# One visit of TensorE for the key-value products of two pairs of heads

## The chip, the cores and the metric

The kernel runs on one core of one Trainium2 chip. The metric is device time in microseconds (us), taken as the median of the timed runs. The profile shows one execution of the program; its engines are named PE (TensorE, the matrix engine; PEld is its loading of the stationary operand), DVE (VectorE), ACT (ScalarE), POOL (GpSimd) and SP (SyncE, which here only issues transfers).

## The reference, cut to what matters

Linear attention is followed by a two-layer network over all tokens:

```
q_s = softmax of q over the 64 numbers of a head
k_s = softmax of k over the 576 keys of a head
kv  = einsum('bhsd,bhse->bhde', k_s, v)          # 64 x 64 per head
x   = einsum('bhsd,bhde->bhse', q_s, kv)         # 8 batches x 576 tokens, 8 heads
h   = x @ w_in
out = (h * clip(h + 3, 0, 6) / 6) @ w_out        # 4608 x 512 -> 2048 -> 512
```

All is float32. There are 8 batches, 8 heads of 64 numbers and 576 keys per batch.

## The kernel before, in words

**Blocks.** The 4608 tokens are worked through in nine blocks of 512 (`j` from 0 to 8). A block's attention gives `x`, kept as a rounded half and a remainder (`split`: ACT casts, DVE subtracts), since a float32 product is made of three products of such halves. Blocks 0 and 1 use the plain first product (`gemm1`); from block 2 on (`FAST`) the first product follows a scheme with seven quarter products (`fast_pair`, one call for two of the sixteen column blocks of `w_in`, so eight "pairs of columns" per block), for which `x_factors` prepares sums of `x` and `fast_weights` once prepares sums of the weights.

**Attention.** A unit of attention is one pair of heads of one block (`attention(j, hp)`, four units per block: 128 rows hold two heads of 64). It is a Python generator of four steps, separated by `yield`: (1) load, take the maximum of each key row (`km`) and make q's softmax on its transposed layout (`q_softmax_t`), ending with a transpose on DVE; (2) spread the maxima: POOL copies the column `km` to a 128x128 tile `kb`, PE transposes it into `pm`, DVE subtracts it from `ke`, ACT takes the exponential, and q is split; (3) `kv_of`: ten products of 64 columns on PE into `pkv` (five chunks of keys, two heads), then DVE divides by the sum of the exponentials, which is a 65th column of the product, and the result is split; (4) six products into `px` give `x`, which `x_factors` copies and splits. The last chunk of keys has 64 rows (`TAIL`), the four others 128. With 576 keys and blocks of 512 tokens, a block needs the `kv` of batch `j - 1` and of batch `j`. There are eight batches, so block 8 has no step (3).

**What sets the order.** The generator `steps` is advanced once per column block in blocks 0 and 1 and twice per pair of columns from block 2 on (in `fast_pair`, at the second and fourth call of `slot`). It runs ahead: during block `j` it does mostly the attention of block `j + 1`. Units come in the order 0, 2, 1, 3, since `x_factors` needs pair 2 for pair 0 and pair 3 for pair 1. From block 1 on PE executes its instructions in the order in which they are written; on the other engines a scheduler sets the order, with priority for the evacuations marked `high_priority`. The second product of an earlier pair of columns (`gemm2`, into `po`) waits in `pend` and is issued in fills of 4, 7, 7 and 6 between the quarter products. Transfers are issued by SP in one queue; among them are the weights of the fast scheme (`w<-wf`), through a ring of twelve half tiles.

**Names in the profile.** The matmul helper has one line, L91, so its groups are told apart by tile: `pkv` (step 3), `px` (step 4), `pm` (transposes, L97), `ph` and `pz` (first product), `po` (second product). L123 and L124 are the two halves of `split`. L353 is the subtraction of the maxima, L340 the POOL copy to `kb`, L215 to L218 the division, L535, L541 and L554 evacuations of the first product.

## Time and profile before

| what | value |
|---|---|
| time, median of 3 runs | 892.73 us (892.33 to 893.6) |
| the profiled execution: first to last instruction | 888.9 us |
| PE busy, share of the span | 858.4 us, 97% |
| PEld, DVE, ACT, POOL busy | 739.2, 614.6, 464.8, 132.9 us |
| products into `pkv` in blocks 1 to 7 | 560 instructions, 28 visits of 20 |
| transposes into `pm` | 24 |

The execution behind the profile has no time of its own beside its span; the span lies 3.8 us below the median of the timed runs, which also hold what comes before the first and after the last instruction. A line of `kv_of` that issues one product stands as two instructions in the profile, so ten products are a visit of 20. Ends of matmuls are modelled by the profile, since they are pipelined; starts are what can be compared. Rows of the timeline merge neighbours of one kind: start, time to the last end, engine, line, tiles, shape, count.

### The profile page before, as it was taken

The numbers are of one execution on the slowest core, as the hardware profiler recorded it, in microseconds if no ns is written. First come the engines' busy times: TensorE is split into PE (matmuls) and PEld (weight loads), VectorE is DVE, ScalarE is ACT, GpSimd is POOL, SyncE is SP. The second block draws the span as 40 slices with busy tenths as digits, with TensorE's granted clock in tenths as the row PEclk, the third lists the DMA queues.
The fourth block names the chain that finished last, engine by engine and source line by source line (L and its number), as shares of the span: only waits on it lengthen the run. The fifth ranks groups of instructions, "written<-read, shape, count | busy, mean of one in ns | idle before, by whom it ended". The sixth has DMA issues, their size and how long they took to land.

```text
span 888.9 us, 15262 instructions
## 1 busy us (share of the span) xinstructions
PE 858.4 (97%) x5380; PEld 739.2 (83%) x5380; DVE 614.6 (69%) x1266; ACT 464.8 (52%) x944; POOL 132.9 (15%) x329
## 2 busy tenths in 40 slices
PE   5799998999999999999999999999999999999998
PEld 3578776787789888888888888888888888889896
DVE  7999867899777766767585757676867565444333
ACT  7998753544445454545454545444554554434333
POOL 5000132021212110202020202021212120100000
PEclk9899999999999999999999999999999999999999
DMA  9992583538487668676777668676755575567541
GB/s 372 413 369 84 125 203 136 180 108 289 161 259 224 219 202 258 216 224 203 228 233 229 209 220 259 200 230 195 256 158 183 161 230 170 167 178 224 170 140 47
DMA packets 98474, 185.19 MB, mean 208 GB/s; under 512 B 9824, under 2 KB 24160, under 8 KB 96352
## 3 DMA queue, kind: packets, MB, share of 16 engines
q1 hardware_dynamic: 96192, 180.03, 62.3%
q0 software_dynamic: 1632, 3.15, 2.0%
q10 hardware_dynamic: 576, 1.05, 0.3%
q8 instruction: 43, 0.70, 0.3%
q14 instruction: 31, 0.25, 0.1%
HBM read 156.93 MB, written 24.12 MB: 204 GB/s over the span
## 4 chain that ended last, share of the span: by engine, by line
PE 83%; DVE 7%; DMA 6%; ACT 2%; issue 1%; POOL 0%; SPq 0%; ACTq 0%; DVEq 0%; POOLq 0%
PE po L91 41%; PE ph L91 33%; PE pz L91 4%; PE px L91 2%; PE pkv L91 2%; DMA w<-v 2%; DMA qt<-in_qf_dram 2%; DVE w L124 1%; DMA out_dram<-ob 1%; DVE v L155 1%; DVE v L149 0%; DMA wf<-w 0%; POOL swap L289 0%; DVE km L267 0%; DVE v L159 0%
## 5 line engine op out<-in xcount | busy, mean ns | idle before, releaser
L91 PE MATMUL po<-w,w 128*128 128x512 f32 x1008 | 260.8, 394 | 0.8 <-ACT w L123 0.8
L91 PEld LDWEIGHTS po<-w,w 128*128 128x128 f32 x1008 | 178.4, 189 | 30.7 <-ACT w L123 1.1
L91 PE MATMUL ph<-x_lo,w 128*128 128x256 f32 (+1 forms) x800 | 152.2, 305 | 2.7 <-DVE x_lo L124 2.3
L91 PEld LDWEIGHTS ph<-w,w 128*128 128x128 f32 x1008 | 133.8, 190 | 11.0 <-DVE second L535 1.4
L91 PE MATMUL ph<-x_hi,w 128*128 128x256 f32 (+1 forms) x592 | 138.4, 338 | 4.4 <-DMA w<-v 3.3
L91 PE MATMUL ph<-w,w 128*128 128x256 f32 x1008 | 140.4, 284 | 1.2 <-DVE second L535 1.2
L91 PEld LDWEIGHTS ph<-x_lo,w 128*128 128x128 f32 x800 | 117.0, 189 | 17.0 <-DVE x_lo L124 2.6
L91 PEld LDWEIGHTS ph<-x_hi,w 128*128 128x128 f32 x592 | 93.3, 191 | 18.8 <-DMA w<-v 3.5
L124 DVE TENSOR_TENSOR w<-g,w 128x512 fp32r<-128x512 f32 x112 | 77.2, 689 | 35.3 <-ACT w L123 35.3
L123 ACT CAST w<-g 128x512 fp32r<-128x512 f32 x112 | 69.4, 619 | 56.7 <-DVE g L541 34.4
L91 PE MATMUL po<-w 128*128 128x512 f32 x336 | 86.7, 394 | 0.1
L91 PEld LDWEIGHTS po<-w 128*128 128x128 f32 x336 | 59.4, 188 | 10.8 <-ACT w L123 0.5
L91 PE MATMUL po<-w,g_hi 128*128 128x512 f32 x256 | 67.4, 401 | 0.9 <-ACT g_hi L123 0.9
L556 ACT ACTIVATE g<-second,three 128x512 f32<-128x512 f32 x56 | 40.5, 724 | 33.9 <-DVE second L554 26.5
L91 PEld LDWEIGHTS po<-w,g_hi 128*128 128x128 f32 x256 | 47.7, 190 | 12.2 <-ACT g_hi L123 1.4
L540 ACT ACTIVATE g<-ph,three 128x256 f32<-128x256 f32 x56 | 26.6, 474 | 57.9 <-PE ph L91 57.9
L541 DVE SCALAR_TENSOR_TENSOR g<-g,ph 128x256 f32<-128x256 f32 x56 | 23.2, 415 | 47.1 <-ACT g L540 47.0
L534 ACT COPY second<-ph 128x256 f32<-128x256 f32 x56 | 20.8, 372 | 63.1 <-PE ph L91 63.1
L557 DVE SCALAR_TENSOR_TENSOR g<-g,second 128x512 f32<-128x512 f32 x56 | 39.0, 697 | 15.3 <-ACT g L556 15.2
L91 PE MATMUL pz<-x_hi,w 128*128 128x256 f32 x336 | 49.5, 283 | 0.0
L535 DVE TENSOR_TENSOR second<-second,ph 128x256 f32<-128x256 f32 x56 | 23.1, 413 | 37.5 <-ACT second L534 37.5
L289 POOL COPY swap<-qr 32x16 f32<-32x16 f32 x112 | 30.6, 273 | 96.4 <-DVE qr L301 92.8
(125 smaller groups left out, 1264.2 us busy)
## 6 DMA issues: line engine op xcount, KB each, us to landing
w<-wf SPq DMA_DIRECT2D x392, 256.0 KB, 3.0
raw<-in_w_dram SPq DMA_DIRECT2D x16, 1024.0 KB, 13.4
out_dram<-ob SPq DMA_DIRECT2D x36, 256.0 KB, 3.3
vt<-in_v_dram SPq DMA_DIRECT2D x28, 325.0 KB, 3.5
wf<-w SPq DMA_DIRECT2D x16, 512.0 KB, 4.7
kt<-in_kT_dram SPq DMA_DIRECT2D x28, 288.0 KB, 3.0
ke<-in_k_dram SPq DMA_DIRECT2D x24, 320.0 KB, 2.9
qt<-in_qf_dram SPq DMA_DIRECT2D x28, 256.0 KB, 3.0
```

The source lines that it names most:

```text
L91: nc.tensor.matmul(out, lhsT, rhs, start=start, stop=stop, skip_group_check=goes_on)
L123: nc.scalar.copy(hi, src)
L124: engine.tensor_sub(lo, src, hi.bitcast(F32))
L155: nc.vector.scalar_tensor_tensor(vu, high, 0xC0000000, m, op0=ALU.bitwise_and, op1=ALU.bitwise_or)
L289: nc.gpsimd.tensor_copy(swap[r : r + QD], stat[o : o + QD])
L534: nc.scalar.copy(second[:, HT:], x)
L535: nc.vector.tensor_add(second[:, HT:], second[:, HT:], y)
L540: nc.scalar.activation(r[:, HT:], x, AF.Relu, bias=three, scale=1.0)
L541: nc.vector.scalar_tensor_tensor(r[:, HT:], r[:, HT:], 6.0, x, op0=ALU.min, op1=ALU.mult)
L556: nc.scalar.activation(r, second, AF.Relu, bias=three, scale=1.0)
L557: nc.vector.scalar_tensor_tensor(r, r, 6.0, second, op0=ALU.min, op1=ALU.mult)
```

## The change

From block 2 on, attention is written for two pairs of heads at a time, (0, 2) and then (1, 3), in the generator `paired`, with eight steps where two units had four each. In the order of the steps: load and softmax of the first pair; its maxima and exponentials, and load and softmax of the second; maxima and exponentials of the second; q of the first transposed and split; `kv` of both pairs in one visit of PE, the second pair 128 columns further in the same tile; `x` of the first; q of the second transposed and split; `x` of the second. In block 2 itself the eight steps are six. The last chunk of keys is used with all 128 rows: the loaded `ke` and `vt` of blocks 2 to 7 already have rows below the 64 keys (the smallest float in k, zeros in v), and in blocks 0 and 1 POOL now writes zeros there. The column of maxima is no longer copied to a tile: PE's transpose reads the column with a step of zero. The sum plus epsilon and its reciprocal are taken once for both pairs. The split halves of `kv` have six buffers where they had five.

```diff
-    def kv_of(j, hp, ke, vt):
+    def kv_of(j, units):
+        n = len(units)
         pkv = ps_a.tile([P, TB], F32, name="pkv", tag="pa")
-        for c in range(NCH):
-            r = slice(0, P if c < NC4 else TAIL)
-            for h in range(2):
-                hs = slice(h * D, (h + 1) * D)
-                mm(pkv[hs, 0 : D + 1], ke[r, c, hs], vt[r, c, h, :], c == 0, c == NCH - 1)
-        rk = att.tile([P, 1], F32, name="rk", bufs=2)
-        nc.vector.tensor_scalar_add(rk, pkv[:, D : D + 1], EPS)
+        for i, (hp, ke, vt) in enumerate(units):
+            for c in range(NCH):
+                for h in range(2):
+                    hs = slice(h * D, (h + 1) * D)
+                    mm(
+                        pkv[hs, i * KVW : i * KVW + D + 1],
+                        ke[:, c, hs],
+                        vt[:, c, h, :],
+                        c == 0,
+                        c == NCH - 1,
+                        i > 0,
+                    )
+        sums = pkv.rearrange("p (i n) -> p i n", n=KVW)[:, 0:n, D]
+        rk = att.tile([P, 2], F32, name="rk", bufs=2)[:, 0:n]
+        nc.vector.tensor_scalar_add(rk, sums, EPS)
         nc.vector.reciprocal(rk, rk)
...
     def k_softmax(j, km, ke, kt):
         nc.scalar.copy(ke[0:TAIL, NC4], pe2[0:TAIL, 0:P])
+        nc.gpsimd.memset(ke[TAIL:P, NC4], 0.0)
...
+    def paired(j, hps):
+        qts, kes, kbs, vts = {}, {}, {}, {}
+        def begin(hp):
...
+            if j < B:
+                km = att.tile([P, 1], F32, name="km", bufs=2)
+                nc.vector.tensor_reduce(km, kt, axis=AX.X, op=ALU.max)
+                kbs[hp] = km.broadcast_to([P, P])
+            q_softmax_t(qts[hp])
+        def exp_k(hp):
+            if j < B:
+                ke = kes[hp]
+                pm = ps_a.tile([P, TB], F32, name="pm", tag="pa")
+                flip(pm[:, 0:P], kbs[hp])
...
+        def turn_q(hp):
+            qT = moe.tile([P, 2 * DM], F32, name="m", tag="v", bufs=3)[:, 0:TB]
+            nc.vector.transpose(qT, qts[hp])
...
+        one, two = hps
+        begin(one)
+        yield
+        exp_k(one)
+        begin(two)
+        yield
+        exp_k(two)
+        yield
+        turned = turn_q(one)
+        if j > FAST:
+            yield
+        if j < B:
+            kv_of(j, [(hp, kes[hp], vts[hp]) for hp in hps])
+            for hp in hps:
+                kv_split(j, hp)
+        yield
+        x_of(one, *turned)
+        if j > FAST:
+            yield
+        turned = turn_q(two)
+        yield
+        x_of(two, *turned)
...
     def steps():
-        for j in range(1, NB):
-            heads = range(NP) if j < FAST else (0, 2, 1, 3)
-            for hp in heads:
-                unit = attention(j, hp)
...
+        for hp in range(NP):
+            for _ in attention(1, hp):
+                yield
+            yield
+        for j in range(FAST, NB):
+            for hps in ((0, 2), (1, 3)):
+                for _ in paired(j, hps):
                     yield
-                next(unit, None)
+                yield
```

The first two places are on PE and DVE. On PE, during block 2, where step (3) of a unit of block 3 stood (`w` and `x_hi`, `x_lo` are operands of the first product, `po` is a fill of the second product), this stood before:

```order
L91 MATMUL po<-w_533,w_1016 128x512 x6
L91 MATMUL ph<-x_lo_311,w_656 128x256 x6
L91 MATMUL po<-w_533,w_1016 128x512 x6
L91 MATMUL pkv<-vt,ke 64x65 x10
L91 MATMUL ph<-w_365,w_656 128x256 x6
L91 MATMUL pz<-x_hi_310,w_716 128x256 x6
L91 MATMUL ph<-x_hi_310,w_716 128x256 x6
```

And now, for both pairs of heads (1, 3):

```order
L91 MATMUL ph<-w_337,w_782 128x256 x6
L91 MATMUL ph<-w_309,w_782 128x256 x6
L91 MATMUL po<-w_593,w_1075 128x512 x7
L91 MATMUL pkv<-vt,ke 64x65 x20
L91 MATMUL ph<-x_lo_315,w_835 128x256 x6
L91 MATMUL po<-w_593,w_1075 128x512
```

Twenty products stand in a row where ten stood, once per two pairs of heads, and they come after the first fill of seven of a pair of columns and not after its fill of six.

On DVE, in the first pair of columns of block 3, between two evacuations of the first product (`second`) and the split of its result (`w`), this stood before (`qt`, `qm` and `m` belong to the softmax of the next unit, `ob` is a store of block 2):

```order
L535 TENSOR_TENSOR second<-second,ph 128x256
L124 TENSOR_TENSOR qT_lo<-m,qT_hi 128x512
L604 TENSOR_SCALAR ob<-po 128x512
L124 TENSOR_TENSOR x_lo_311<-v,x_lo_311 128x256
L307 STREAM_TRANSPOSE m<-qt 128x512
L297 TENSOR_REDUCE qm<-qt 128x16
L541 SCALAR_TENSOR_TENSOR g<-g,ph 128x256
L554 TENSOR_TENSOR second<-second,ph 128x256
L290 TENSOR_TENSOR qm<-qm,swap 128x16
L124 TENSOR_TENSOR w_957<-g,w_957 128x512
```

And now:

```order
L571 TENSOR_TENSOR second<-second,ph 128x256
L124 TENSOR_TENSOR kv_lo_0_3508<-kv,kv_hi_0_3507 128x128
L124 TENSOR_TENSOR kv_lo_2_3512<-kv,kv_hi_2_3511 128x128
L640 TENSOR_SCALAR ob<-po 128x512
L577 SCALAR_TENSOR_TENSOR g<-g,ph 128x256
L124 TENSOR_TENSOR w_964<-g,w_964 128x512
L399 STREAM_TRANSPOSE m<-qt 128x512
L590 TENSOR_TENSOR second<-second,ph 128x256
```

Ahead of the evacuation into `g` (L541, now L577) stood five other operations after `second`; now three stand there, two of them on 128x128, and the transpose has moved behind the split.

The third place is on DVE in the next pair of columns of block 3, from the split of its first result (`w_1075` in the changed program) to that of its second. Before, at the next like place, the work beside the first product was that of two softmaxes alone:

```order
L124 TENSOR_TENSOR w_957<-g,w_957 128x512
L299 TENSOR_TENSOR qt<-qt,qm 128x512
L297 TENSOR_REDUCE qm<-qt 128x16
L557 SCALAR_TENSOR_TENSOR g<-g,second 128x512
L527 TENSOR_TENSOR first<-first,pz 128x256
L301 TENSOR_REDUCE qr<-qt 128x16
L124 TENSOR_TENSOR w_1016<-g,w_1016 128x512
```

And now:

```order
L124 TENSOR_TENSOR w_1075<-g,w_1075 128x512
L320 TENSOR_TENSOR qt<-qt,qr 128x512
L314 TENSOR_TENSOR qt<-qt,qm 128x512
L590 TENSOR_TENSOR second<-second,ph 128x256
L124 TENSOR_TENSOR qT_lo<-m,qT_hi 128x512
L124 TENSOR_TENSOR x_hi_314<-v,x_hi_314 128x256
L124 TENSOR_TENSOR x_lo_315<-v,x_lo_315 128x256
L124 TENSOR_TENSOR w_309<-v,w_309 128x256
L563 TENSOR_TENSOR first<-first,pz 128x256
L124 TENSOR_TENSOR w_337<-v,w_337 128x256
L316 TENSOR_REDUCE qr<-qt 128x16
L593 SCALAR_TENSOR_TENSOR g<-g,second 128x512
```

The splits of `x_factors` (`x_hi`, `x_lo`, `w_309`, `w_337`) now stand among the softmaxes of the two next pairs of heads, ahead of L593, whose result the split into `w` waits for.

More of the change, by code (lines that the diff above doesn't have):

```diff
@@ L305, in q_softmax_t @@
         nc.vector.tensor_mul(qs, qs, across(qr))
-        qT = moe.tile([P, 2 * DM], F32, name="m", tag="v", bufs=3)[:, 0:TB]
-        nc.vector.transpose(qT, qt)
-        return qT
     def attention(j, hp):
-        early = j < 2
         if not j:
@@ L357, in attention @@
-        if early:
-            pool, tag = (ps_a, "pa") if j else (ps_o, "po")
-            tp = pool.tile([P, TB], F32, name="tp", tag=tag)
-            for c in range(NC4):
-                flip(tp[:, c * P : (c + 1) * P], qt[:, c].rearrange("p h d -> p (h d)"))
-            if j:
-                qT = att.tile([P, TB], F32, name="qT", tag="qT_hi")
-            nc.scalar.copy(qT, tp)
-        else:
-            qT_hi = att.tile([P, TB], F32R, name="qT_hi")
-            qT_lo = att.tile([P, TB], F32R, name="qT_lo")
-            split(qT_hi, qT_lo, qT)
@@ L369, in attention @@
[L369 to L375 removed]
+            kt = att.tile([P, S], F32, name="kt", bufs=1)
+            nc.sync.dma_start(kt, kT[j, hp])
+            ke = att.tile([P, NCH, P], F32, name="ke", bufs=2)
+            vt = att.tile([P, NCH, 2, D + 1], F32, name="vt", bufs=2)
+            nc.sync.dma_start(vt, v[j, hp])
+            qt = att.tile([P, TB], F32, name="qt", bufs=2)
+            nc.sync.dma_start(qt, q[j, hp])
@@ new lines, in attention @@
+            qt = qt.rearrange("p (c h d) -> p c h d", c=NC4, h=2)
+        km = att.tile([P, 1], F32, name="km", bufs=2)
+        ks = k_softmax(j, km, ke, kt)
+        next(ks)
+        q_softmax(qt, j == 1, nc.vector if j else nc.gpsimd)
+        yield
+        next(ks, None)
+        pool, tag = (ps_a, "pa") if j else (ps_o, "po")
+        tp = pool.tile([P, TB], F32, name="tp", tag=tag)
+        for c in range(NC4):
+            flip(tp[:, c * P : (c + 1) * P], qt[:, c].rearrange("p h d -> p (h d)"))
@@ L378, in attention @@
+        if j:
+            qT = att.tile([P, TB], F32, name="qT", tag="qT_hi")
+        nc.scalar.copy(qT, tp)
+        yield
+        kv_of(j, [(hp, ke, vt)])
+        yield
         pool, tag = (ps_a, "pa") if j else (ps_h, "ph")
@@ L390, in attention @@
                     mm(px[:, c], kv_lo, qT_hi[:, c], False, True)
-        if j < FAST:
-            x_hi, x_lo = x_block(j)
-            split(x_hi[:, hp, :], x_lo[:, hp, :], px)
-            if j == 1:
-                kv_split(j, hp)
-        else:
-            x_factors(j, hp, px)
+            x_factors(j, hp, px)
+        one, two = hps
[9 more added lines that the diff above has]
+            yield
+        if j < B:
+            kv_of(j, [(hp, kes[hp], vts[hp]) for hp in hps])
+            for hp in hps:
+                kv_split(j, hp)
+        yield
[5 more added lines that the diff above has]
+        x_of(two, *turned)
     HT = TB // 2
@@ L636, in steps @@
     def steps():
-        for j in range(1, NB):
-            heads = range(NP) if j < FAST else (0, 2, 1, 3)
-            for hp in heads:
-                unit = attention(j, hp)
-                for step in range(4):
-                    next(unit, None)
-                    if j == FAST and step == 3 and hp != 3:
-                        continue
+        for hp in range(NP):
[5 more added lines that the diff above has]
+                for _ in paired(j, hps):
                     yield
-                next(unit, None)
+                yield
     step = steps()
```

99 lines of the change are left out of this document (45 added, 54 removed).

## The prediction

> **What bounds the kernel now.** I read the page first: busy shares, the slices, and the chain that ended last.
>
> ```profile
> span 888.9 us, 15262 instructions
> PE 858.4 (97%) x5380; PEld 739.2 (83%) x5380; DVE 614.6 (69%) x1266; ACT 464.8 (52%) x944; POOL 132.9 (15%) x329
> ...
> PE   5799998999999999999999999999999999999998
> ...
> DVE  7999867899777766767585757676867565444333
> PE 83%; DVE 7%; DMA 6%; ACT 2%; issue 1%; POOL 0%; SPq 0%; ACTq 0%; DVEq 0%; POOLq 0%
> ```
>
> PE is full but for the first slices, and 83% of the chain is PE. A share of busy time hides how stages differ, so I read the stages next (columns: stretch, then busy us and count of PE, PEld, DVE, ACT, POOL, the granted clock, DMA share, GB/s).
>
> ```profile
> 0.00:33.00 33.00, 17.83 (x124) 11.52 (x124) 27.92 (x51) 27.01 (x39) 11.32 (x19) 0.89 0.97 385
> 33.00:144.00 111.00, 102.79 (x504) 80.61 (x504) 99.52 (x159) 83.40 (x166) 14.13 (x27) 0.97 0.69 217
> ...
> 430.00:522.70 92.70, 92.41 (x638) 82.04 (x637) 64.42 (x144) 46.61 (x100) 15.77 (x44) 1.00 0.70 223
> ```
>
> Up to 144 us DVE and ACT feed PE and it waits for them; from there on PE sets the pace (92.41 of 92.70 us) and DVE has some 28 us to spare in a block. So in blocks 2 to 8 what PE is spared is spared at the end, as long as nothing else gets late. The waits of PE confirm it (columns: total, times, longest):
>
> ```profile
> PE ph L91 <- DMA w<-v: 3.3, 2, 3.0
> ...
> PE ph L91 <- DVE second L535: 1.2, 1, 1.2
> ...
> PE po L91 <- ACT w L123: 0.8, 1, 0.8
> ...
> PE ph L91 <- ACT second L534: 0.4, 1, 0.4
> PE ph L91 <- DVE g L541: 0.3, 1, 0.3
> ```
>
> The last four belong to blocks 2 and later, 2.7 us in all.
>
> **The visit to `pkv`.** Its price is read from starts. The timeline of PE with no visit, then with one at the same place between a fill and the products after it:
>
> ```profile
> 300.27 1.55 PE L91 MATMUL po<-w,w 128*128 128x512 f32 x6
> 301.66 0.86 PE L91 MATMUL ph<-w,w 128*128 128x256 f32 x6
> 302.36 0.87 PE L91 MATMUL pz<-x_hi,w 128*128 128x256 f32 x6
> ...
> 310.91 1.55 PE L91 MATMUL po<-w,w 128*128 128x512 f32 x6
> 312.39 0.95 PE L91 MATMUL pkv<-vt,ke 128*64 128x65 f32 x20
> 313.27 0.98 PE L91 MATMUL ph<-w,w 128*128 128x256 f32 x6
> 314.08 0.88 PE L91 MATMUL pz<-x_hi,w 128*128 128x256 f32 x6
> ```
>
> Six `po` take 1.39 us to the next start without a visit and 1.48 before one: entry 0.09. The visit takes 312.39 to 313.27, 0.88. The six products behind it take 0.81 and not 0.70: exit 0.11. Sum 1.08. Where the 0.88 goes, narrower stretches of the same view and the view by tile show:
>
> ```profile
> 312.39 0.28 PE L91 MATMUL pkv<-vt,ke 128*64 128x65 f32 x2
> ...
> 312.50 0.40 PE L91 MATMUL pkv<-vt,ke 128*64 128x65 f32 x8
> ...
> 312.79 0.29 PE L91 MATMUL pkv<-vt,ke 128*64 128x65 f32 x4
> ...
> 313.01 0.33 PE L91 MATMUL pkv<-vt,ke 64*64 64x65 f32 x4
> ...
> L91 PE MATMUL pkv<-vt,ke x20: 218/222/271, 312.4 to 313.1; 128*64 128x65 f32 x16, 64*64 64x65 f32 x4
> ...
>   issue: 7.1, 21
> ```
>
> The two heads run side by side, so twenty instructions are ten couples. The first takes 0.11 (312.39 to 312.50). The last four of the sixteen with 128 rows begin at 312.79, so five couples lie between 312.50 and 312.79: 0.058 each. Couple eight would begin at 312.85 and the 64-row ones begin at 313.01: 0.16 and not 0.058, so the change of shape costs 0.10. The two 64-row couples take 0.26 to the exit and not 0.12: 0.05 for a first couple again, 0.10 on the way back to 128x128. "issue", 21 times in all visits, says that PE waits there for nothing else that the trace shows.
>
> **What the change does to it.** A visit for two pairs is one first couple, 18 at 0.058 and a last one with its way out at 0.16: 0.11 + 1.04 + 0.16 = 1.31, plus entry and exit 0.20: 1.51. Two visits are 2.16 now. Saved 0.65 per two pairs; blocks 2 to 7 have two such visits each, twelve: **7.8 us**. The fifth chunk's added rows cost nothing by this count: 64-row products last 0.22 as the others do, and the rows are loaded already. In blocks 0 and 1 a visit loses only its change of shape, 0.15; the four in block 1's attention give **0.6**, the four before 33 us nothing, since PE is busy there 17.83 of 33 us. The one visit waits for the exponentials of both pairs, and so does what is behind it on PE, in order. They are asked for two and more steps earlier, a step being half a pair of columns, 5.3 us (10.55 us for a pair of columns without attention, below), so I take no wait.
>
> The order of DVE moves the other stalls. At the start of block 3 PE waits for a split:
>
> ```profile
> 345.97 0.68 DVE L604 TENSOR_SCALAR ob<-po 128x512 f32<-128x512 f32 x1
> ...
> 346.90 0.70 DVE L307 STREAM_TRANSPOSE m<-qt 128x512 f32<-128x512 f32 x1
> 347.54 0.69 DVE L297 TENSOR_REDUCE qm<-qt 128x16 f32<-128x512 f32 x1
> 348.14 0.41 DVE L541 SCALAR_TENSOR_TENSOR g<-g,ph 128x256 f32<-128x256 f32 x1
> ...
> 349.04 0.87 PE L91 MATMUL ph<-x_hi,w 128*128 128x256 f32 x6
> 350.68 0.74 PE L91 MATMUL po<-w,w 128*128 128x512 f32 x2 [0.77 <-ACT w L123]
> ```
>
> L541 stands behind a store, a transpose and a maximum of the next unit. In the changed order the transpose and that softmax are behind it, so this wait should go. At the start of block 2 the same waits, 1.2 and 0.4, pull the clock down as well:
>
> ```profile
> 252.00:258.00 6.00, 4.76 (x26) 4.46 (x26) 4.89 (x12) 2.59 (x6) 1.77 (x5) 0.72 0.81 233
> ...
> 254.94 1.48 PE L91 MATMUL pz<-x_hi,w 128*128 128x256 f32 x6
> 256.22 1.48 PE L91 MATMUL ph<-x_hi,w 128*128 128x256 f32 x6
> ```
>
> Six `pz` take 1.28 to the next start, where six products took 0.70 above. PE's 4.76 us at a clock of 0.72 would be 3.4 at full clock: 1.3 lost. The waits and the clock are 4.0 us that can go. At block 2 a store of the previous block still stands ahead of L571, so I take **3.0**, between 0 (each wait replaced by another) and 4.0.
>
> The Trainium skill, page "TensorE: Matmul & The Clock Gate", Part 1, has the clock fall back to half only after an idle window of about 3.4 us. By that the short waits at block 2 would cost no clock, 1.3 us less could be won, and the sum below would be 882.6. This case's trace does not agree: 0.72 after waits of 1.2 and 0.4.
>
> **Edits taken at nothing.** The POOL copies (24) and twelve additions and reciprocals less on DVE free engines that PE covers; if DVE were the bound, 12 x 0.31 = 3.7 us more would come (the rows of `rk` are 152 and 156 ns). Transposing a column with step zero is not in this trace:
>
> ```profile
> L97 PE MATMUL pm<-ident,kb 128*128 128x128 f32 x24 | 6.5, 271 | 0.0
> L97 PEld LDWEIGHTS pm<-ident,kb 128*128 128x128 f32 x24 | 3.3, 139 | 1.0
> ```
>
> Nearest is the same load from a full tile, 139 ns under running products: 0. If the load took three times as long and nothing covered it, 24 x 0.28 = 6.7. I take 0, since the same number of elements is read. A gain is excluded: the load is hidden now. The eight zero fills on POOL (15% busy) go between its transfers `w<-v`, one of which a PE wait of 3.0 names; with the new order of the first two blocks, where DVE and ACT lead, I take 0 and keep 3 us either way.
>
> SP's queue is re-dealt: the key transfers of two pairs come one step apart and the second waits for the first's maximum, with weight fetches behind it. The ring holds twelve of them, 12/7 of a pair of columns or 18 us of work, against one softmax, some 5 us.
>
> Sum, against the profiled execution: 888.9 - 7.8 - 0.6 - 3.0 = 877.5. The median of the runs lies 3.8 above that span and I carry it over: **881.3 us**.
>
> **Rivals.**
>
> (a) *Only the visits pay.* Other waits replace those at the block starts, and the new order of the DVE-led start costs up to 3: 892.7 - 8.4 = 884.3, to 887.3. For it: the scheduler re-deals those blocks, and before 144 us PE idles 23 us (33.00 - 17.83 and 111.00 - 102.79), so an order there can be worth some of it. Against it: the order at the start of block 3 above.
>
> (b) *DVE becomes the bound where `x_factors` meets two softmaxes* (the third place of the order). Stretches of a pair of columns each, the last without attention:
>
> ```profile
> 580.52:592.24 11.72, 11.72 (x89) 10.24 (x88) 10.04 (x23) 6.28 (x12) 3.29 (x14) 1.00 0.66 211
> 592.24:603.66 11.42, 11.42 (x74) 10.29 (x73) 8.32 (x21) 5.96 (x15) 3.65 (x7) 1.00 0.68 214
> 826.15:836.70 10.55, 10.55 (x69) 9.50 (x68) 3.92 (x9) 3.97 (x8) 0.00 (x0) 1.00 0.58 175
> ```
>
> The fullest two hold 18.4 us of DVE in 23.1 and PE has no wait there. The change packs in about as much, the two softmaxes and the six splits of `x_factors` closer together, and without a visit two pairs of columns last as little as 21.1 (2 x 10.55). If the split for the second product gets late by d, PE waits d twelve times; the gain of 11.4 is gone at d = 0.95, and at 1.5 the time is 892.7 + 6.6 = 899. Against it: 21.1 - 18.4, some 2.7 us of room.
>
> By the Trainium skill, page "TensorEngine Tiling (Array Packing)", PSUM Bottleneck, packing speeds TensorE but not the evacuation, which may then become the bottleneck. That speaks for (b); the rows show no such wait yet.
>
> (c) *The change of shape is not what is paid.* Should the 0.1 steps at entry, at 64 rows and at exit come from something per unit, two pairs would still cost 2.16 and only the block starts change: 889.7 to 892.7. The step-zero load at its upper end lands in the same place as (a), 888.
>
> **How the numbers follow.** Forecast 0.54 (879 to 884), rival (a) 0.27 (884 to 889), (c) 0.08, (b) 0.11, most of it slower than before. The likeliest time is 881.3. Two cases in ten left out, one at each end: 877.0 (all 4.0, and the start 3 better: 877.3) to 889.5. What a measurement of this kernel can tell from no change is about 0.2%, 1.8 us: faster 0.85 (forecast, (a) and half of (c)), same 0.07 (the rest of (c), a small (b)), slower 0.08.
>
> **What would show it.** Right: in blocks 2 to 7 twelve visits of 40 instructions, 1.31 us from first start to the next product, all of 128 rows, 0.058 a couple; at the start of blocks 2 and 3 no wait of PE for `w` or `second`, and a clock of 1.00 from 252 to 258. Wrong: couples of the second pair slower than the first's; a wait of PE for `w` or `first` in the second and third pair of columns of a block; `pm` with a load far over 139 ns; a start of block 2 later than 244 us.

## The result: slower by 1.6%

The changed kernel takes 906.79 us (median of 4 runs, 905.3 to 908.56), the kernel before 892.53 us on the same chip (4 runs, 891.38 to 893.6). The ratio is 1.0164, 95% interval 1.0145 to 1.0183: 14.3 us slower, where 881.3 us and a range of 877.0 to 889.5 had been predicted. The profiled execution took 906.11 us, 1.8 more than its span.

The page of the changed kernel, with the chain of waits at its end:

```profile
span 904.3 us, 15151 instructions
...
PE 854.4 (94%) x5380; PEld 735.8 (81%) x5380; DVE 613.7 (68%) x1242; ACT 464.6 (51%) x944; POOL 139.9 (15%) x313
...
PE 58%; DVE 19%; DMA 11%; ACT 6%; issue 3%; POOL 2%; SPq 0%; POOLq 0%; ACTq 0%
```

PE is busy 4.0 us less than before (858.4), and yet the span is 15.4 us longer: PE idles 49.9 us and not 30.5. The chain says who it waits for. PE was 83% of it and is 58%; DVE went from 7% to 19%, DMA from 6% to 11%. The waits of PE name two evacuations that were on no such list before (in all, times, longest):

```profile
PE ph L91 <- DVE second L590: 7.6, 6, 1.7
PE ph L91 <- ACT first L560: 7.5, 6, 2.3
```

`first` is the first copy of a pair of columns, `second` the last sum; the next products go into the PSUM tiles that they free.

Where the time lies, by blocks (the stretches begin and end with the first product of a block, so their lengths are block times), blocks 3 and 5 of the changed kernel:

```profile
336.57:432.19 95.62, 91.64 (x638) 81.22 (x637) 65.19 (x141) 46.77 (x100) 16.52 (x40) 1.00 0.69 217
...
527.48:626.62 99.14, 95.15 (x638) 84.39 (x637) 65.28 (x141) 46.63 (x100) 15.65 (x40) 0.97 0.67 206
```

A block of 92.7 us became one of 95 to 99 with the same DVE work (65 us against 64.4). Block 2 begins at 244.60 (244.00 before) and is 1.15 shorter; blocks 3 to 6 are 15.0 us longer in all (385.8 against 370.8), block 7 is 1.0 longer. That is the whole 15.4.

The mean length of each of the eight pairs of columns over blocks 3 to 6, from the starts of their first products, shows where (us; the last line is the best version found below and serves as the clean length, that is, the length with next to no wait):

```
pair of columns        1      2      3      4      5      6      7      8    sum of 4 blocks
before             11.35  12.24  11.36  11.72  11.35  11.72  11.36  11.60     370.8
after              12.88  13.63  11.38  10.74  12.88  11.37  12.94  10.63     385.8
run 13 (best)      12.88  11.40  10.66  10.98  12.88  11.37  10.63  10.89     366.8
```

The visits are in pairs 1 and 5. The loss is in pair 2 (2.23 us each against the clean length), pair 7 (2.31) and pair 3 (0.72).

**The visit itself** did what was predicted. Timeline of PE in the changed kernel, and the transposes of the column with step zero by tile:

```profile
295.03 1.39 PE L91 MATMUL pkv<-vt,ke 128*64 128x65 f32 x40
296.34 0.98 PE L91 MATMUL ph<-x_lo,w 128*128 128x256 f32 x6
297.16 0.62 PE L91 MATMUL po<-w,w 128*128 128x512 f32 x2
...
L97 PEld LDWEIGHTS pm<-ident,km x24: 133/134/138, 154.0 to 670.0; 128*128 128x128 f32 x24
```

40 instructions, 1.31 us from the first start to the next product, six products behind it 0.82: the predicted 1.31 and 0.11 of exit. The load of the step-zero column takes 134 ns, the copied tile's took 139.

**The second pair of columns.** First the issues of SP's queue in block 3 of the changed kernel, then ACT, then PE:

```profile
342.94 0.33 SPq L374 DMA_DIRECT2D ke<-in_k_dram  x1
343.33 0.42 SPq L376 DMA_DIRECT2D vt<-in_v_dram  x1
343.85 0.37 SPq L374 DMA_DIRECT2D ke<-in_k_dram  x1
344.28 0.42 SPq L376 DMA_DIRECT2D vt<-in_v_dram  x1
...
345.95 0.34 SPq L643 DMA_DIRECT2D out_dram<-ob  x1
...
348.83 0.59 ACT L470 COPY v<-px 128x512 f32<-128x512 f32 x1 [0.52 <-PE px L91]
351.14 0.60 ACT L642 ACTIVATE ob<-po 128x512 f32<-128x512 f32 x1 [1.72 <-DMA out_dram<-ob]
351.63 0.40 ACT L123 CAST x_hi<-v 128x256 fp32r<-128x256 f32 x1
...
352.75 0.72 ACT L592 ACTIVATE g<-second,three 128x512 f32<-128x512 f32 x1
353.38 0.36 ACT L560 COPY first<-ph 128x256 f32<-128x256 f32 x1
...
353.79 0.98 PE L91 MATMUL ph<-w,w 128*128 128x256 f32 x6 [1.24 <-ACT first L560]
```

The visit at 342.06 releases the keys and values of both pairs of heads at once, and the scheduler sends the four loads that waited for those buffers (2 x 320 and 2 x 325 KB, 1.29 MB) right away, ahead of the previous block's stores. There are two output buffers. The first store goes out at 345.95 and frees its buffer 5.2 us later; ACT, which must evacuate the third part of the block, stands until 351.14, and `x_hi`, q's rounding, `x_lo`, an activation and then the copy that PE needs are behind it in order. Before the change no load stood there (two rows of ACT in block 4 of the kernel before):

```profile
442.04 0.60 ACT L606 ACTIVATE ob<-po 128x512 f32<-128x512 f32 x1 [2.26 <-DMA out_dram<-ob]
...
443.67 0.36 ACT L524 COPY first<-ph 128x256 f32<-128x256 f32 x1
```

ACT waited here too, but only until 442.04, 0.84 us into the second pair of columns (begun at 441.20), with two instructions between it and the copy; in the changed kernel the wait ends 1.80 us into it in block 3 (351.14 against 349.34) and 2.40 us in block 4, with four.

**The third and seventh pair of columns.** DVE, POOL and PE, block 3 of the changed kernel:

```profile
362.15 0.69 DVE L124 TENSOR_TENSOR w<-g,w 128x512 fp32r<-128x512 f32 x1
362.75 1.23 DVE L320 TENSOR_TENSOR qt<-qt,qr 128x512 f32<-128x512 f32 x1
363.90 1.23 DVE L314 TENSOR_TENSOR qt<-qt,qm 128x512 f32<-128x512 f32 x1
365.05 0.41 DVE L590 TENSOR_TENSOR second<-second,ph 128x256 f32<-128x256 f32 x1
...
363.39 1.19 POOL L480 TENSOR_TENSOR v<-v 128x256 f32<-128x256 f32 x1
364.54 1.18 POOL L481 TENSOR_TENSOR v<-v 128x256 f32<-128x256 f32 x1
...
365.51 1.70 PE L91 MATMUL ph<-w,w 128*128 128x256 f32 x12 [0.94 <-DVE second L590]
```

The sum that PE waits for stands behind the end of one softmax (L320) and the subtraction of the next (L314), and both last 1.23 us, while POOL makes the four differences of `x_factors`. From 244 to 720 us these two kinds of instruction, 40 in all, have a median of 0.69 us where no difference of POOL runs beside them; of the 15 that meet one, twelve last 1.10 to 1.25 and three 0.65 to 0.69. Before the change one of 42 met one.

### The profile page after: what moved, and what is told of

Same layout as the page of the kernel before. It is cut to its first block, busy times and chain, and to the rows that moved or that the text cites. A ratio compares the mean times of both kernels' runs of the same rounds, so it can differ in the third digit from the quotient of the medians.

```text
span 904.3 us, 15151 instructions
## 1 busy us (share of the span) xinstructions
PE 854.4 (94%) x5380; PEld 735.8 (81%) x5380; DVE 613.7 (68%) x1242; ACT 464.6 (51%) x944; POOL 139.9 (15%) x313
## 4 chain that ended last, share of the span: by engine, by line
PE 58%; DVE 19%; DMA 11%; ACT 6%; issue 3%; POOL 2%; SPq 0%; POOLq 0%; ACTq 0%
PE po L91 29%; PE ph L91 23%; DMA qt<-in_qf_dram 4%; PE pz L91 3%; DMA out_dram<-ob 3%; DVE w L124 3%; POOL swap L304 2%; DMA w<-v 2%; PE pkv L91 2%; DVE qt L314 1%; DVE v L155 1%; ACT w L123 1%; DMA wf<-w 1%; DVE v L159 1%; DVE qm L312 1%
## 5 line engine op out<-in xcount | busy, mean ns | idle before, releaser
L91 PE MATMUL ph<-w,w 128*128 128x256 f32 x1008 | 144.2, 286 | 15.3 <-DVE second L590 7.6
L91 PEld LDWEIGHTS ph<-w,w 128*128 128x128 f32 x1008 | 134.4, 191 | 27.9 <-DVE second L590 10.8
L91 PEld LDWEIGHTS ph<-x_hi,w 128*128 128x128 f32 x592 | 92.7, 190 | 18.5 <-DMA w<-v 6.2
L124 DVE TENSOR_TENSOR w<-g,w 128x512 fp32r<-128x512 f32 x112 | 79.9, 713 | 36.5 <-ACT w L123 36.5
L478 POOL TENSOR_TENSOR v<-v 128x256 f32<-128x256 f32 x14 | 10.4, 745 | 356.6 <-ACT v L470 167.6
L577 DVE SCALAR_TENSOR_TENSOR g<-g,ph 128x256 f32<-128x256 f32 x56 | 23.4, 419 | 60.9 <-ACT g L576 60.7
L593 DVE SCALAR_TENSOR_TENSOR g<-g,second 128x512 f32<-128x512 f32 x56 | 38.9, 695 | 21.9 <-ACT g L592 21.9
## 6 DMA issues: line engine op xcount, KB each, us to landing
raw<-in_w_dram SPq DMA_DIRECT2D x16, 1024.0 KB, 14.3
```

The source lines that it names most:

```text
L91: nc.tensor.matmul(out, lhsT, rhs, start=start, stop=stop, skip_group_check=goes_on)
L124: engine.tensor_sub(lo, src, hi.bitcast(F32))
L478: nc.gpsimd.tensor_sub(t1, x12, x11)
L577: nc.vector.scalar_tensor_tensor(r[:, HT:], r[:, HT:], 6.0, x, op0=ALU.min, op1=ALU.mult)
L593: nc.vector.scalar_tensor_tensor(r, r, 6.0, second, op0=ALU.min, op1=ALU.mult)
```

## The experiments

Two theories stood after this: **DVE crowded where softmaxes meet the splits of `x_factors`** (theory 1: pairs 3 and 7, rival b of the prediction) and **loads ahead of stores** (theory 2: pair 2; in runs 3 and 4 it was still the looser one that SP's queue makes ACT wait for an output buffer). A third, that the paired visit's own burst of divisions and splits delays the rest, was kept as the rival. Each run was timed beside the kernel before on its chip; lengths of pairs of columns are means over blocks 3 to 6 of the profiled execution, as in the table. Line numbers shift between kernels, the tiles' names do not.

### Runs 1 and 2: the two small parts alone

Run 1, on the kernel before:

```diff
-            r = slice(0, P if c < NC4 else TAIL)
-                mm(pkv[hs, 0 : D + 1], ke[r, c, hs], vt[r, c, h, :], ...)
+                mm(pkv[hs, 0 : D + 1], ke[:, c, hs], vt[:, c, h, :], ...)
         nc.scalar.copy(ke[0:TAIL, NC4], pe2[0:TAIL, 0:P])
+        nc.gpsimd.memset(ke[TAIL:P, NC4], 0.0)
```

> The kernel before with one edit: every chunk of keys is used with 128 rows (POOL writes zeros below the 64 keys in blocks 0 and 1). My theory (the visits pay as predicted, the loss is elsewhere): each of 28 visits loses its change of shape, some 0.15 us; the 24 behind the DVE-led start count, so 3.6 to 4.2 us less, about 888.5 us. Rival (c) of the prediction (the change of shape is not what is paid): no change, 892.5. If the zero fills disturb the first two blocks, the start of block 2 moves later than 244.0.

Measured: 887.60 us against 892.07, ratio 0.995 (0.9935 to 0.9966). 4.5 us for 28 visits, 0.16 each, and in the profile a pair of columns with a visit and no wait went from 11.72 to 11.57: the change of shape is what is paid, and rival (c) falls.

Run 2, on the kernel before:

```diff
-                kb = att.tile([P, P], F32, name="kb", bufs=1)
-                nc.gpsimd.tensor_copy(kb, km.broadcast_to([P, P]))
+                kb = km.broadcast_to([P, P])
```

> The kernel before with one edit: PE transposes the column of maxima with a step of zero, POOL copies nothing. My theory: no change within 1.5 us, 892.5, and the transpose's weight load stays near 139 ns. Rival (the step-zero load is slow, or the column is free later than the copied tile and holds something up): a load two or three times as long and up to 6.7 us more.

Measured: 893.05 us, ratio 1.000 (0.9981 to 1.0018). No change.

### Runs 3, 4 and 8: the steps dealt otherwise

The changed kernel's eight steps (b: load and softmax, e: exponentials, t: q turned and split, kv: the visit, x: product and `x_factors`; 1 and 2 the two pairs of heads) and three other orders, from block 3 on:

```
after   b1 | e1 b2 | e2 | t1    | kv    | x1    | t2 | x2
run 3   b1 | e1    | b2 | e2    | t1 kv | x1 t2 | x2 | -
run 4   b1 | e1    | b2 | e2 t1 | kv    | x1    | t2 | x2
run 8   b1 | e1 b2 | e2 | t1    | kv    | x1 t2 | x2 | -
```

> The changed kernel, visits paired as they are, with its eight steps in blocks after the second dealt otherwise: softmax of the first; exponentials of the first; softmax of the second; exponentials of the second; q of the first and the visit; x of the first and q of the second; x of the second; nothing. So the two softmaxes stand a pair of columns apart and the six splits of x_factors stand a step ahead of the next softmax. Theory 1 (DVE is crowded where two softmaxes and six splits share two pairs of columns, the prediction's rival b): the stalls of 19.5 us on PE behind block 2 fall below 6 and the time is 881 to 886. Theory 2 (SP's queue: key transfers and stores wait on one another and ACT waits for an output buffer, which makes the first copy late in the second pair of columns of a block): the stalls there, some 8 us, stay, 890 to 893. Theory 3 (the paired visit itself gives DVE and ACT a burst of divisions and splits that delays what follows): nearly no change, 900 or more.

Measured: 908.48 us, ratio 1.0181 (1.0163 to 1.0198). The time is the one that theory 3 expected, but none of the theories had it whole. Pair 7 fell from 12.94 to 10.94, as theory 1 has it, and pair 2, which theory 1 didn't explain, rose from 13.63 to 15.72. The trace says why: in blocks 5 and 6 PE waits a second time in pair 2, 1.88 and 2.51 us, for `second`, and in block 5 that sum stands behind three instructions that run beside POOL's differences at 1.25, 1.22 and 0.95 us, so the crowd of theory 1 had moved there; in blocks 3 and 4 the waits for `first` (2.71 and 2.04 us) bring the clock down as well.

> The changed kernel with one thing moved: the softmax of the second pair of heads one step later (and its exponentials one later, with q of the first). x of the second stays where it is, ahead of the next first softmax. Theory 1: the pair of columns with the splits and two softmaxes loses one of them; the stalls in the third and seventh pair of columns (9.4 us) mostly go, those in the second shrink: 888 to 897. Theory 2: as in the run before, the stalls of the second pair of columns stay; 895 to 900. Theory 3: no change, 905.

Measured: 910.17 us, ratio 1.0197 (1.0164 to 1.0230). Pair 7 at 12.15, pair 2 at 13.41: with the softmaxes apart and the splits where they were, a little is won in these pairs and nothing in the time. That too is theory 3's number (905) and not that of the other two.

> The changed kernel with x of the second pair of heads one step earlier (q of the second turned in the step of the first's x, then x, then nothing); the two softmaxes stay one step apart. It tells the six splits from the second softmax. In the fourth run, with the softmaxes two steps apart and the splits where they were, the seventh pair of columns stayed at 12.3, 14.4, 12.2, 11.1 us (the changed kernel: 12.2, 12.7, 12.8, 14.4). If the splits beside the first softmax are what is too much: 10.7 to 11.3 here. If two softmaxes are too much by themselves: 12 or more. The second pair of columns stays long in either case, and the time near 897 to 905.

Measured: 909.68 us, ratio 1.0185 (1.0151 to 1.0220). Pair 7 at 10.80 with both softmaxes still together; pair 2 at 14.54. So in pair 7 the splits beside a softmax are too much, not two softmaxes. The time, expected at 897 to 905, is longer, since pair 2 rose as in run 3 (a second wait for `second` in blocks 5 and 6, 1.46 and 2.19 us). None of the three orders brought pair 2 down by more than 0.22, as theory 2 says.

### Runs 5, 6 and 7: the loads away from the stores

Run 5, on the changed kernel; `tc.issue_after` puts what its block issues behind the last store in the order of the same queue, and adds no other wait:

```diff
+    def load(to, source):
+        if not stores:
+            nc.sync.dma_start(to, source)
+            return
+        with tc.issue_after(stores[-1].ins):
+            nc.sync.dma_start(to, source)
...
-                nc.sync.dma_start(kes[hp], ...)
+                load(kes[hp], ...)
...
-                nc.sync.dma_start(vts[hp], ...)
+                load(vts[hp], ...)
```

> The changed kernel with one rule more for SP's queue: the loads of keys and values (ke, vt) are issued behind the last store of the block before, not ahead of it. Nothing else moves. Theory 2 in its new form (the paired visit frees both pairs' buffers at once; their four loads, 1.29 MB, go out right ahead of the stores; ACT's third store waits 1.7 to 2.9 us until 14.6 to 15.8 us into the block for an output buffer where it waited until about 12 before the change, and the first copy of the second pair of columns is behind it): that wait ends near 12 us again, the second pair of columns in blocks 3 to 6 goes from 12.7, 13.4, 15.3, 13.0 us to some 11.7, 7.6 us less in all and the clock dips with it: 897 to 900 against 906.8. The stalls of the seventh pair of columns stay. Rival (DVE and ACT are short of time there whatever the stores do): the second pair of columns stays within 0.5 us of what it was, 905 to 908.

Measured: 898.53 us, ratio 1.0070 (1.0044 to 1.0097), 8.3 us less than the changed kernel. Pair 2 went from 13.63 to 11.49 and pair 3 from 11.38 to 10.67; pair 7 stayed (12.92). ACT in block 3 of this run, whose second pair of columns begins at 348.22:

```profile
348.00 0.60 ACT L670 ACTIVATE ob<-po 128x512 f32<-128x512 f32 x1 [0.81 <-DMA out_dram<-ob]
...
350.86 0.36 ACT L588 COPY first<-ph 128x256 f32<-128x256 f32 x1
```

The wait for the buffer ends before the pair of columns begins; the store issued at 344.82 needs 3.2 us now, and in blocks 4 to 6 ACT has no such wait. Theory 2 in this form is shown.

> The steps dealt as in the third run, and the loads of keys and values behind the stores. By theory 2 in its new form the second pair of columns of blocks 3 to 6 (15.7, 15.2, 16.2, 15.8 us there) falls to about 11.7, some 16 us and block 2's 2 us: 889 to 893 against 908.5. Rival: above 903.

Measured: 892.27 us, ratio 0.9993 (0.9974 to 1.0012); 16.2 us less than run 3, which has the same steps.

Run 7 takes run 3's steps, a pair of columns later against the block:

```diff
+            yield            # one more idle step in each half of block 2
```

> The steps dealt as in the third run, but all of them two steps (one pair of columns) later from block 3 on, by one idle step more in each half of block 2: the visit and its loads then come in the second and sixth pair of columns, behind the stores. By theory 2 in its new form the stores are free of the loads and ACT's wait ends near 12 us into the block; the stalls of 20.4 us fall to 5 or less: 884 to 890. Rival (the order of steps is right only as it was against the block's start; x is ready later by a pair of columns): waits of the first product of a block for its splits, 895 or more.

Measured: 894.57 us, ratio 1.0019 (1.0003 to 1.0036). The visit is now in pairs 2 and 6 (12.88 each, as elsewhere), so the loads are out of the way; stalls moved to pairs 3 and 7 (12.70 and 12.14). Between the two expectations, nearer to the rival's number though not by its mechanism: PE waits there for `second`, not for the first product's splits.

### Runs 9 and 10: is it POOL, and do steps reach DVE's order?

Run 9, on run 5, leaves out POOL's differences, so its output is not the network's and only its times are used:

```diff
-        nc.gpsimd.tensor_sub(t1, x12, x11)
-        nc.gpsimd.tensor_sub(t2, x22, t1)
-        nc.gpsimd.tensor_sub(t3, x22, x12)
-        nc.gpsimd.tensor_sub(t4, x21, t2)
+        t1, t2, t3, t4 = x12, x22, x11, x21
```

> The kernel of the fifth run (loads behind the stores), with POOL's four differences in x_factors left out: the splits take plain quarters of x instead, so the products of the fast scheme are made of other numbers, with the same count of splits and products. It tells whether POOL slows DVE. In the changed kernel DVE's subtraction and multiplication of q (128x512) last 1.21 us (median) where POOL's differences run at the same time and 0.69 where they do not; 15 of 40 are caught, 1 of 42 in the kernel before. If POOL is what doubles them: all near 0.69, some 1.5 us less DVE work ahead of the late evacuation in the seventh pair of columns, whose stall (2.8, 2.2, 1.8 us in the fifth run) falls to 1 or less; span near 887. If not (they are slow for their place or their operands): still 1.2 and the stall as it was, 892.

Run 5 first, DVE, POOL and PE in pair 7 of block 3:

```profile
406.15 1.25 DVE L320 TENSOR_TENSOR qt<-qt,qr 128x512 f32<-128x512 f32 x1
407.32 1.21 DVE L124 TENSOR_TENSOR w<-g,w 128x512 fp32r<-128x512 f32 x1
408.45 1.21 DVE L314 TENSOR_TENSOR qt<-qt,qm 128x512 f32<-128x512 f32 x1
409.58 0.41 DVE L618 TENSOR_TENSOR second<-second,ph 128x256 f32<-128x256 f32 x1
...
406.80 1.17 POOL L508 TENSOR_TENSOR v<-v 128x256 f32<-128x256 f32 x1
407.94 1.17 POOL L509 TENSOR_TENSOR v<-v 128x256 f32<-128x256 f32 x1
...
410.04 1.70 PE L91 MATMUL ph<-w,w 128*128 128x256 f32 x12 [2.66 <-DVE second L618]
```

Then run 9, the same place, without the differences:

```profile
408.38 0.41 DVE L613 TENSOR_TENSOR second<-second,ph 128x256 f32<-128x256 f32 x1
...
408.87 0.63 DVE L314 TENSOR_TENSOR qt<-qt,qm 128x512 f32<-128x512 f32 x1
...
410.01 0.69 DVE L320 TENSOR_TENSOR qt<-qt,qr 128x512 f32<-128x512 f32 x1
```

Measured: 888.43 us in one run, span 886.7; all 40 instructions last 0.63 to 0.69, pair 7 is 11.37 on average. That POOL's differences nearly double them is shown. That the stall shrinks for this alone is not: with the differences gone the scheduler also placed `second` ahead of L314 and L320.

Run 10 puts a pause ahead of the first softmax, on run 5 (`- | b1 | e1 b2 | e2 t1 | kv | x1 | t2 | x2`).

> The kernel of the fifth run (loads behind the stores) with a step's pause after x of the second pair of heads, so that the six splits and POOL's differences are over when the next softmax begins; the exponentials of the second then come with q of the first in one step. My theory: with the splits apart from the first softmax the seventh pair of columns of blocks 3 to 6 (13.6, 14.5, 12.8, 10.8 us) falls to about 11, the third stays near 10.7 and the second near 11.3: a span of 883 to 886 and a median of 885 to 889, below the kernel before. Rival (the work only moves: the eighth or fifth pair of columns is then the crowded one, with exponentials that end right ahead of the visit): waits of pkv or of the first product there, 893 or more.

Measured: 896.79 us, ratio 1.0043 (1.0024 to 1.0061). Pair 7 at 13.26, no better than 12.92. In block 3 DVE's order there is the one of run 5 (L320, the split, L314, then `second`), although the softmax is written a step later. So the means was wrong; that the scheduler sets the order by when data is there, and that q's transfers (issued at 395.30 and 398.34, the place is at 406.60) were early enough, is my reading and was not tested by itself.

### Run 11: another order with the pause

> The same rule for the loads; the steps are: pause; softmax of the first; its exponentials; softmax of the second; its exponentials and q of the first; the visit; x of the first and q of the second; x of the second. The softmaxes are two steps apart and no splits stand beside them, but the visit is a step later and three things follow it in two steps. If evenness of DVE over the pairs of columns is all that matters: 884 to 888. If what follows the visit is crowded then (q of the second together with x of the first, as in the sixth run's sixth pair of columns, 11.9 to 12.6 us): 888 to 893.

Measured: 901.89 us, ratio 1.0077 (1.0053 to 1.0101), more than either expectation. Its stalls are small and many (pairs 2, 6 and 7 at 13.04, 12.17 and 12.13); I didn't follow it further.

### Runs 12, 13 and 14: the order on DVE set by rule

Run 12, on run 5:

```diff
-            split(to[n][:, 0, i], to[n][:, 1, i], src)
+            splits.append(split(to[n][:, 0, i], to[n][:, 1, i], src))
...
-            q_softmax_t(qts[hp])
+            with tc.issue_after(splits[-1].ins):     # once there are any
+                q_softmax_t(qts[hp])
```

> The kernel of the fifth run (loads behind the stores) with a second rule, for DVE's order: a softmax of q is issued behind the last of the six splits of x that are written ahead of it. The steps stay as the change has them. In the fifth run's trace the softmaxes stand in the seventh pair of columns ahead of the evacuation that PE waits for, and two of their three long operations there run beside POOL's differences at 1.2 us; in the tenth run a pause in the steps did not move them, since their place comes from when their data is there. My theory (this crowd is what is left): the seventh pair of columns of blocks 3 to 6 (13.6, 14.5, 12.8, 10.8 us) falls to 11 or less, all of q's subtractions and multiplications but a few last 0.69, the stalls behind block 2 fall from 10.9 to 4, span 882 to 886, median 885 to 889. Rival (the softmaxes are then late for q's transposition and the visit): a wait of pkv or px in the fifth or first pair of columns, 893 or more.

Measured: 888.77 us, ratio 0.9952 (0.9938 to 0.9966): faster than the kernel before. Pair 7 is at 10.63, and none of the 40 instructions meets POOL's differences (eleven multiplications for `g`, which stand behind the evacuation, now do). A smaller stall came up in pairs 4 and 8 (11.36, 11.44). DVE and PE in block 4 of this run:

```profile
464.15 0.74 DVE L390 TENSOR_REDUCE km<-kt 128x1 f32<-128x576 f32 x1
...
464.89 0.69 DVE L124 TENSOR_TENSOR w<-g,w 128x512 fp32r<-128x512 f32 x1
465.49 0.69 DVE L320 TENSOR_TENSOR qt<-qt,qr 128x512 f32<-128x512 f32 x1
466.09 0.42 DVE L622 TENSOR_TENSOR second<-second,ph 128x256 f32<-128x256 f32 x1
...
466.56 0.62 PE L91 MATMUL ph<-w,w 128*128 128x256 f32 x3 [0.81 <-DVE second L622]
```

Run 13 adds to run 12 that the maximum of the keys and the softmax are issued behind the last `second` written before them, and takes run 4's steps:

```diff
+            evacuated.append(nc.vector.tensor_add(second[:, 0:HT], second[:, 0:HT], y))
...
+                with tc.issue_after(evacuated[-1].ins):
+                    nc.vector.tensor_reduce(km, kt, axis=AX.X, op=ALU.max)
...
+                with tc.issue_after(splits[-1].ins), tc.issue_after(evacuated[-1].ins):
+                    q_softmax_t(qts[hp])
```

> The kernel of the twelfth run with one rule more for DVE's order: the maximum of the keys and the softmax of q are issued behind the last evacuation (second) of the pair of columns written before them, and the second softmax is written one step later, the exponentials of the second with q of the first. The twelfth run's fourth and eighth pair of columns last 11.36 and 11.44 us where 10.65 is bare: PE waits 0.3 to 1.0 us there for that evacuation, which stands behind a subtraction from ke, a maximum of kt, a split and a multiplication of q. My theory (order on DVE is all that is left in these blocks): both fall to 10.8 or less, blocks 3 to 6 from 371.1 to 366 us in all, the median from 888.8 to 882 to 886. Rival (DVE's work does not fit between the visits in any order): the wait shows in another pair of columns, 888 or more.

Measured: 884.47 us, ratio 0.9921 (0.9891 to 0.9951), the best version: 7.6 us below the kernel before on the same chip, 22 below the change. Blocks 3 to 6 take 366.8 us. Pairs 4 and 8 are at 10.98 and 10.89, a little above the 10.8 expected. The paired visit with all its divisions and splits is still there, so theory 3 falls. Its page:

```profile
span 880.0 us, 15174 instructions
...
PE 848.0 (96%) x5380; PEld 733.5 (83%) x5380; DVE 609.5 (69%) x1242; ACT 465.9 (53%) x944; POOL 124.8 (14%) x313
```

DVE has 609.5 us of work, nearly the changed kernel's 613.7; its order differs. The profiled execution is the fastest of the six, 881.80 us, and of the 8.9 us by which its span is shorter than the one before 3.5 lie ahead of block 2 (begun at 240.50), 2.8 in block 2 and 4.0 in blocks 3 to 6, and behind them it is 1.4 longer. So from block 2 on the gain over the kernel before is some 5 us; the earlier start is not explained (over all kernels it lies between 240.5 and 249.8).

Run 14 is run 12 without run 5's rule.

> The kernel of the twelfth run without the rule for the loads: softmaxes behind the splits, keys and values loaded ahead of the stores again. If the two causes are separate and add up: the second pair of columns of blocks 3 to 6 is long again (13 us and more on average, against 11.5), the seventh stays near 10.7, and the time is 888.8 + 8 = 896 to 899. If the order of DVE alone would do (the softmaxes out of the way let ACT and DVE catch up): 891 or less.

Measured: 900.05 us, ratio 1.0080 (1.0053 to 1.0107), a little above the 896 to 899 expected. Pair 2 is long again (14.11), pair 7 stays at 10.63. The causes are separate: from 906.8, the rule for the loads alone gives 8.3, the rule for DVE alone 6.7, both together 18.0. The sum is 15.0, and the intervals are too wide to tell the two apart; in blocks 3 to 6 of the profiled executions it is 11.1, 4.5 and 14.7, which add up within 1 us.

## Why the prediction was wrong, point by point

**The visit, 7.8 us: right in its parts, about 1 us high in all.** 1.31 us inside, 0.09 entry and 0.11 exit are in the trace. Pairs of columns without a wait give some 1.1 us a block (block 3: 4 x 11.21 + 4 x 11.72 before, 2 x 12.77 + 2 x 11.23 + 4 x 10.66 after), 6.5 in six blocks. Run 1 paid 4.5 us for the change of shape where "0.15" a visit had been counted. With nearly all stalls out of the way (run 13) the kernel is 7.6 us below the one before; the sum had 11.4, and its forecast of 881.3 lies 3.2 below that run's median.

**"SP's queue is re-dealt": the step that failed first.** It was taken at nothing: the ring of weights was weighed against one softmax, and the loads' place against the block's stores was not looked at, although key transfers that "come one step apart" for two pairs mean that one visit frees two pairs' buffers. What the runs showed in its place: the loads go ahead of the stores, the store's 3.2 us become 5.2, ACT waits for the buffer and PE for ACT's `first`. It cost 8.3 us (run 5), and the prediction's own sign of being wrong, a wait of PE for `first` in the second pair of columns, is what came. The rows that would have told it were in the trace of before, where ACT waits for `out_dram<-ob` in the second pair of columns of blocks 3 to 6 (2.61, 2.26, 1.78 and 1.80 us). In block 3 the wait already cost PE something:

```profile
349.52 0.60 ACT L606 ACTIVATE ob<-po 128x512 f32<-128x512 f32 x1 [2.61 <-DMA out_dram<-ob]
350.02 0.61 ACT L123 CAST w<-g 128x512 fp32r<-128x512 f32 x1
```

PE's 0.77 at 350.68 is for this `w`. The prediction put it down to what stands ahead of DVE's L541, but L541 ended at 348.55, and ACT, in order, could not begin the cast before 350.02.

**Rival (b), given 0.11: the right place, the wrong test.** It named `x_factors` against two softmaxes, though PE's wait came for `second` and not for the split that it priced. It was set aside by an average over two pairs of columns, "18.4 us of DVE in 23.1", some 2.7 us of room. In the changed kernel two such pairs (6 and 7 of block 3) would still pass: 8.73 + 11.06 = 19.8 us of DVE where 21.9 is the clean length. But the work is uneven:

```profile
397.65:408.88 11.23, 11.23 (x74) 10.19 (x73) 8.73 (x20) 6.19 (x15) 3.28 (x12) 1.00 0.70 224
408.88:421.54 12.66, 10.93 (x70) 9.49 (x69) 11.06 (x23) 6.58 (x16) 4.61 (x8) 1.00 0.49 143
```

The second has 11.06 us of DVE where 10.63 is clean, and lasts 12.66 with PE 1.7 us short. What decides is what stands ahead of the evacuation at its hour, in order, and run 13 does nearly the same work with no such wait. Two things made it worse than the sum allowed for: the scheduler put two softmaxes there, and three long instructions there (run 5's rows) cost 1.2 us instead of 0.69 beside POOL. The prediction took POOL as 15% busy and free. The trace of before had the sign of it, in other instructions. A split of 128x256 lasts 0.41 us alone, but this one took 721 ns on average:

```profile
L124 DVE TENSOR_TENSOR x_hi<-v,x_hi 128x256 fp32r<-128x256 f32 x28 | 20.2, 721 | 26.4 <-ACT x_hi L123 26.4
```

From 244 to 720 us 20 of its 21 meet a difference of POOL, and these last 0.61 to 0.96.

By the Trainium skill, page "SBUF — State Buffer", section "Who interferes with whom", a VectorE instruction with two SBUF inputs contends with a GpSimd instruction that reads SBUF, and the ports they share are an exclusive lock. The traces agree: in run 5 the split issued at 407.32 ends at 408.53, 0.56 after POOL's L508 ended at 407.97, POOL's next then ends 0.58 after that, and the few reductions that meet one, with one input, keep 0.67 to 0.69 us.

**The waits at the start of blocks 2 and 3, 3.0 us: not won.** The clock from 252 to 258 us is 1.00 as predicted (0.72 before), and of the waits of 1.24 and 0.44 a 0.24 is left. But block 2 has new ones of 0.64, 0.47 and 1.00 us further on and is 1.15 us shorter, no more than its two visits were to pay (2 x 0.65), and block 3 has the wait of 1.24 us for `first` where the 0.77 stood.

**The start, 3 us either way: right here, too narrow for the runs.** Block 2 begins at 244.6 us and not at 244.0, but in the profiled executions of the sixteen kernels between 240.5 and 249.8. What sets it is open; it doesn't explain the loss, which lies behind it.

**Step-zero maxima at 0: right** (run 2: 1.000; 134 ns a load). **The wait of the one visit for the exponentials of both pairs, taken at nothing: right**, PE waits for `pkv` only once, for 3.2 us, ahead of block 2.

## What to carry to other kernels

When two units are merged, look at what they release together: the transfers that were spaced by two visits go out in one burst, and whatever stands behind them on that queue, here the stores and through them ACT, pays for it. Room on an engine read as an average says nothing on an in-order queue; list what stands ahead of each evacuation that the bounding engine waits for, in the new order. Where a scheduler places work by when its data is there, moving it in the program may move nothing; a rule of order on the queue did, and with the loads behind the stores it turned a loss of 1.6% into a gain of 0.8%, of which some 0.6% lie behind the start of block 2.

## What the runs showed of the hardware

**DVE beside POOL.** A 128x512 DVE instruction with two SBUF operands: 0.69 us alone, up to 1.25 beside POOL's differences; the few 128x512 reductions that meet one, with one operand, stay at 0.67 to 0.69, and the sums into `second`, whose other operand is in PSUM, at 0.38 to 0.42 (15 of them in the changed kernel). In the kernel before q's softmaxes hardly met the differences (one of 42), which hid the price that the splits already paid.

**The clock after a wait.** In the changed kernel PE waits 2.34 us in block 5 (until 545.97) and 1.81 us in block 4 (until 450.08), and only the first brings the clock down. Stretches of 3.41 us around them, PE's busy time second, the granted clock third from the end:

```profile
542.17:545.58 3.41, 1.46 (x10) 1.12 (x8) 1.33 (x3) 2.25 (x6) 0.00 (x0) 1.00 0.81 298
545.58:548.99 3.41, 3.02 (x10) 2.73 (x11) 3.18 (x7) 1.74 (x5) 0.00 (x0) 0.50 0.93 290
...
446.59:450.01 3.42, 1.68 (x11) 1.29 (x9) 1.66 (x4) 2.58 (x6) 0.00 (x0) 1.00 0.89 319
450.01:453.42 3.41, 3.34 (x20) 3.04 (x21) 3.36 (x7) 1.32 (x4) 0.81 (x2) 1.00 0.98 337
```

Between 230 and 880 us eleven of the sixteen traces have such a dip, fifteen in all. Each lasts 3.41 us at 0.50, so a busy PE loses 1.7 us, and where a trace has two they begin 18, 28, 28 and 56 times 3.413 us apart. The clock is thus set on a grid of 3.41 us, and the traces with a dip show where the grid lies. What counts is the idle time of PE in the stretch of the grid just ended (above, 3.41 - 1.46 = 1.95 and 3.42 - 1.68 = 1.74). Of the twelve stretches with 1.84 us of it or more all were followed by a dip, of those with 1.61 or less none, of the twelve between (1.65 to 1.81) three. So two short waits in one stretch add up (1.24 and 0.44 at the start of block 2 before the change: 1.68, and a dip), and an edge can split a longer one (run 5's 2.66 us until 410.04: 1.81 in one stretch, and no dip).

Block 5, with two dips (545.58 and 607.02), is longer by 6.4 us than before, its neighbours by 2.5 to 3.2. By the Trainium skill, page "TensorE: Matmul & The Clock Gate", Part 1, the clock comes down after an idle window of about 3.4 us. The traces have the length of the window, but it need not be idle throughout, and where page and trace differ the trace decides.

**A store behind loads.** The same 256 KB took 5.2 us from its issue to the free buffer behind 1.29 MB of loads and 3.2 us without them.
